# V in 32 KB runs: two kv heads of four batches in one tile, 64 stationary columns, 0/1 masks on P

## The chip, the cores and the metric

The kernel runs on one core of a Trainium2 chip. The metric is the device time of one execution in microseconds; each figure is the median of several executions. Five engines work side by side and wait for one another through semaphores: TensorE (PE in the profile, its weight loads PEld), VectorE (DVE), ScalarE (ACT), GpSimd (POOL) and SyncE (SP). SP issues nearly all of this kernel's transfers in program order; 16 DMA engines carry them out.

## The reference: one decode step of attention beside an MLP

Four sequences (B = 4) have one new token each, with D = 576. The result is `x + A(xn) + B(xn)`, `xn` being the layer norm of `x`.

A is attention over the last W = 2048 of 8192 cached positions, with 32 query heads, 16 kv heads (each serves rep = 2 query heads) and 128 numbers per head:

```
q = xn @ wq                       # 4 x 32 heads x 128
scores = q . k * 128**-0.5        # over 2048 positions
p = softmax(scores)
o = p @ v                         # 4 x 32 x 128
A = o.reshape(4, 4096) @ wo
```

B is `x1 + gelu(layernorm(x1) @ w3) @ w4` with F = 4608. Its first part, which shifts h = gelu(layernorm(x) @ w1) along the sequence before `@ w2`, shifts everything out, as there is one position only, so w1 and w2 are not read.

What must be read is 33.6 MB of K, 33.6 MB of V, 4.7 MB each of wq and wo, and 5.3 MB each of w3 and w4, all in bf16: 87.2 MB in all.

## The kernel before, in words

**Tiles and buffers.** The pool `big` has four buffers of 32 KB per partition, 4 MB each. In turn they hold wq, the K tiles, w3, the V tiles and the end of w4. The pool `kt` has two buffers of 16 KB per partition, `pz` one and `wo` two. A load into a buffer waits, on SP, until the last reader of what the buffer held is done, and every later load stands behind it in SP's queue.

**K and the scores.** Eight K tiles come in, 4 MB each; a partition's row is one run of 32 KB. DVE transposes each in blocks of 32 x 32 (L297), PE multiplies with the queries (L304), and scores of all heads and positions stand in four PSUM banks, `S[0..3]`, one row per (kv head, batch, query head) and 512 columns each.

**Softmax (L309 to L356).** DVE takes the maximum (L316 to L318). ACT makes the exponentials in eight instructions of 256 columns, into the f32 tile `E`, with row sums on the way (L321). DVE takes the reciprocal of the sum (L325, L326) and multiplies it with a mask that says to which batch a row belongs (`rdm`, L328). Then, for each of four pieces of 16 columns, `E` is multiplied with the four columns of `rdm`, three times on DVE (L342) and once on ACT (L340), which gives one copy for each batch, normalized, with zeros in the other batches' rows (`prs`, bf16). PE transposes these (L346), and DVE (L354) and ACT (L351) copy the result from PSUM to `PZ`. `PZ` holds, for each kv head, 64 chunks of 8 columns (4 batches x 2 query heads).

**V.** A V tile holds two kv heads. Each head is one DMA of 2 MB (L122): a partition is a (position block, batch), 32 blocks of 64 positions by 4 batches, so its row is a run of 64 x 128 bf16 = 16 KB. `v_compute(h)` (L384) makes 16 matmuls per head, each with 32 stationary columns of `PZ` (4 chunks x 8 columns) and 512 moving columns of V (4 chunks x 128). They go to four column tiles of 32 in turn; a column tile is a group of 32 PSUM partitions. The blocks on the diagonal, where the chunk of P meets the same chunk of V, are the ones wanted. `head_out(h)` adds up the four diagonal blocks with the 0/1 columns of `diag` (L413 once, L415 three times).

**Behind V.** `transpose_sum` (L425, L427) transposes the sum, adding up over partitions on the way. After every fourth head `select` rearranges four heads' outputs with the matrix `pick` (L436, eight matmuls) and four pairs of small DVE operations (L443, L444), and `project` multiplies them with a group of rows of wo (L395, 16 matmuls). In the loop over v (L545 on) PE's order is written out by hand: `run_projects` (the project of the group before), `v_compute(v)`, then `transpose_sum` and perhaps `select` of head v - 1. SP's order: four V tiles and two wo groups before the softmax, then one V tile after each second head, the third and fourth wo group behind v = 5 and v = 9, and last w4's remaining rows in five DMAs (`w_end`, L482).

**The end.** The last select, the last project, and w4's last rows (L504, four column tiles) go to three accumulators; `sums` and `perm` (L566 to L572) bring them together, and `fin` (L579) goes out.

Of the kernel before, what the change touches and what calls it, by code (L numbers as in the profile page):

```python
# [8 lines left out]
ACT = mybir.ActivationFunctionType  # L9
ALU = mybir.AluOpType  # L10
AX = mybir.AxisListType
BF16 = mybir.dt.bfloat16
F32 = mybir.dt.float32
# [7 lines left out]
def kernel(  # L21
# [30 lines left out]
    NCH = W // G  # L52
    NG = P // G
    GK = G // B
    NY = 4
    CP = 16
    NP = NCH // CP
    assert NCH * GK == 512
# [12 lines left out]
    v_win = A_v_cache[:, :, Sk - W:Sk, :]  # L71
# [46 lines left out]
    def v_load(pair):  # L118
        t = big.tile([P, 2, NCH, Dh], BF16, tag="big", name=f"v{pair}")
        for i in range(2):  # L120
            h = 2 * pair + i
            nc.sync.dma_start(out=t[:, i, :, :].rearrange("p c d -> p (c d)"),  # L122
                              in_=v_win[:, h].rearrange("b (p c) d -> p b (c d)", p=G))
            V_tiles[h] = t[:, i, :, :]
# [5 lines left out]
    wo_src = A_wo.rearrange("(g p x) n -> p g (x n)", p=P, x=XR)  # L130
# [42 lines left out]
    xn_f = const.tile([B, D], F32)  # L173
# [27 lines left out]
    mask = const.tile([P, B], F32)  # L201
    nc.vector.tensor_reduce(out=mask[:], in_=ident[:].rearrange("p (h b r) -> p b h r", b=B, r=rep), op=ALU.add, axis=AX.XY)
# [105 lines left out]

    def softmax():  # L309

        E = ktp.tile([P, NCH, NG, GK], F32, tag="kt", name="E")
        mx = const.tile([P, NG], F32)
        nb = const.tile([P, 1], F32)
        sm = const.tile([P, 2 * NG], F32)
        for g in range(NG):
            nc.vector.reduce_max(out=mx[:, g:g + 1], in_=S[g][:], axis=AX.X)  # L316
        nc.vector.reduce_max(out=nb[:], in_=mx[:], axis=AX.X)
        nc.vector.tensor_scalar_mul(out=nb[:], in0=nb[:], scalar1=-scale)  # L318
        for g in range(NG):
            for x in range(2):  # L320
                nc.scalar.activation(out=E[:, :, g, x:GK:2].rearrange("p (c l) q -> p c q l", l=2),  # L321
                                     in_=S[g][:, 256 * x:256 * (x + 1)].rearrange("p (c q l) -> p c q l", q=4, l=2),
                                     func=ACT.Exp, bias=nb[:], scale=scale, accum_out=sm[:, 2 * g + x:2 * g + x + 1])
        rd = const.tile([P, 1], F32)
        nc.vector.tensor_reduce(out=rd[:], in_=sm[:], op=ALU.add, axis=AX.X)  # L325
        nc.vector.reciprocal(out=rd[:], in_=rd[:])  # L326
        rdm = const.tile([P, B], F32)
        nc.vector.tensor_scalar_mul(out=rdm[:], in0=mask[:], scalar1=rd[:])  # L328

        PZ = pzp.tile([P, Hkv, NCH, B * rep], BF16, tag="pz", name="PZ")  # L330
        HC = CP // 2
        prs = ktp.tile([P, NP, CP, NG, GK, B], BF16, tag="kt", name="prs")
        for piece in range(NP):
            c0 = piece * CP
            pr = prs[:, piece]
            for b in range(B):
                src = E[:, c0:c0 + CP, :, :].rearrange("p c g k -> p (c g k)")
                dst = pr[:, :, :, :, b].rearrange("p c g k -> p (c g k)")
                if b == 3:
                    nc.scalar.mul(out=dst, in_=src, mul=rdm[:, b:b + 1])  # L340
                else:
                    nc.vector.tensor_scalar_mul(out=dst, in0=src, scalar1=rdm[:, b:b + 1])  # L342
            for half in range(2):
                tp = ps_s.tile([P, HC, P], BF16, tag="S", name=f"pt{piece}{half}")
                for cc in range(HC):
                    nc.tensor.transpose(out=tp[:, cc, :],  # L346
                                        in_=pr[:, half * HC + cc, :, :, :].rearrange("p g k b -> p (g k b)"),
                                        identity=ident[:])
                c1 = c0 + half * HC
                if half:  # L350
                    nc.scalar.copy(out=ap_of(PZ, c1 * B * rep, [[NCH * B * rep, Hkv], [B * rep, HC], [1, B * rep]]),  # L351
                                   in_=ap_of(tp, 0, [[B * rep, Hkv], [P, HC], [1, B * rep]]))
                else:
                    nc.vector.tensor_copy(out=ap32(PZ, c1 * B, [[NCH * B, Hkv], [B, HC], [1, B]]),  # L354
                                          in_=ap32(tp, 0, [[B, Hkv], [NH * B // 2, HC], [1, B]]))
        return PZ  # L356


    NI = 4
    NB = B * rep  # L360
    sel = const.tile([P, NB], F32)
    nc.vector.tensor_reduce(out=sel[:], in_=ident[:].rearrange("p (q m) -> p m q", m=NB), op=ALU.add, axis=AX.X)
    diag = const.tile([P, NI], F32)
    nc.vector.tensor_reduce(out=diag[:], in_=ident[:].rearrange("p (j i m) -> p i j m", i=NI, m=NB), op=ALU.add,
                            axis=AX.XY)

    pick = const.tile([P, XR, 2, P // XR], BF16)
    for j in range(2):
        nc.vector.tensor_copy(out=pick[:, :, j, :], in_=ident[:].rearrange("p (m x) -> p x m", x=XR))

    half = const.tile([P, 2], F32)
    nc.vector.tensor_reduce(out=half[:], in_=ident[:].rearrange("p (q j m) -> p j q m", j=2, m=16), op=ALU.add, axis=AX.XY)
    O_tiles = {}

    def v_compute(h):
        bank = ps_o.tile([P, NI * Dh], F32, tag="O", name=f"O{h}")
        vn = V_tiles.pop(h)
        g0, m = divmod(h, NM)
        hp = 4 * (m % 4) + 2 * (m // 4) + g0
        ns = NCH // (NI * NG)  # L380
        for s in range(ns):
            for j in range(NG):
                c0 = (s * NG + j) * NI
                nc.tensor.matmul(out=bank[G * j:G * j + G, :],  # L384
                                 lhsT=PZ[:, hp, c0:c0 + NI, :].rearrange("p c m -> p (c m)"),
                                 rhs=vn[:, c0:c0 + NI, :].rearrange("p c d -> p (c d)"),
                                 start=(s == 0), stop=(s == ns - 1), skip_group_check=True)
        O_tiles[h] = bank
# [11 lines left out]
    NO = 4  # L400

    def load_wo(g2):
        wo_tiles[g2] = wop.tile([P, XR, D], BF16, tag="wo", name=f"wo{g2}")
        nc.sync.dma_start(out=wo_tiles[g2][:].rearrange("p x n -> p (x n)"), in_=wo_src[:, g2, :])
# [3 lines left out]
    def head_out(h):  # L408


        bank = O_tiles.pop(h)
        osum = ktp.tile([P, Dh], F32, tag="kt", name=f"osum{h}")
        nc.vector.tensor_scalar_mul(out=osum[:], in0=bank[:, 0:Dh], scalar1=diag[:, 0:1])  # L413
        for i in range(1, NI):
            nc.vector.scalar_tensor_tensor(out=osum[:], in0=bank[:, i * Dh:(i + 1) * Dh], scalar=diag[:, i:i + 1],  # L415
                                           in1=osum[:], op0=ALU.mult, op1=ALU.add)

        g4, o = divmod(h, NO)

        def transpose_sum():  # L420
            if o == 0:
                OT = ps_tp.tile([P, NO * NB * (1 + XR)], F32, tag="tp", name=f"OT{g4}")
                groups[g4] = OT, small.tile([P, NO, rep, B], BF16, tag="on", name=f"on{g4}")
            OT, on = groups[g4]
            nc.tensor.matmul(out=OT[:, NB * o:NB * o + NB], lhsT=osum[:], rhs=sel[:], start=True, stop=True,  # L425
                             skip_group_check=True)
            nc.vector.tensor_copy(out=on[:, o].rearrange("p r b -> p b r"),  # L427
                                  in_=OT[:, NB * o:NB * o + NB].rearrange("p (b r) -> p b r", r=rep))

        def select():  # L430
            if o < NO - 1:
                return
            OT, on = groups.pop(g4)
            T = OT[:, NO * NB:].rearrange("p (x n) -> p x n", x=XR)
            for x in range(XR):
                nc.tensor.matmul(out=T[0:32, x, :], lhsT=pick[:, x, :, :].rearrange("p j m -> p (j m)"),  # L436
                                 rhs=on[:].rearrange("p o r b -> p (o r b)"),
                                 start=(x == 0), stop=(x == XR - 1), skip_group_check=True)
            onx = small.tile([P, XR, B], BF16, tag="onx", name=f"onx{g4}")
            tmp = small.tile([32, NO, XR, B], F32, tag="tmp", name=f"tmp{g4}")  # L440
            for q in range(NO):
                n = NB * q
                nc.vector.tensor_scalar_mul(out=tmp[:, q], in0=T[0:32, :, n + B:n + 2 * B], scalar1=half[0:32, 1:2])  # L443
# [93 lines left out]
    PZ = softmax()  # L537

    with tc.manual_schedule(engines={mybir.EngineType.PE}):
# [5 lines left out]
        for v in range(Hkv):  # L545
            run_projects()
            v_compute(v)
# [4 lines left out]
            head_out(v)  # L552

            if v in (5, 9):
                load_wo((v + 3) // 4)
            if v % 2 and v // 2 + NV0 < Hkv // 2:
                v_load(v // 2 + NV0)
# [7 lines left out]
        sums = ktp.tile([P, DH], F32, tag="kt", name="sums")  # L565
# [45 lines left out]
```

## Time and profile before

| | |
|---|---|
| median of three runs | 213.44 us (213.19 to 213.72) |
| span of the profiled execution, first to last instruction | 212.0 us; the median lies 1.4 us above it |
| HBM read | 87.17 MB, 411 GB/s over the span |
| busy PE, DVE, ACT | 98.4, 128.2, 17.4 us (46, 60, 8%) |
| last K tile's transposes | end at 121.4 us |
| softmax, from the last scores to the first V matmul | 123.4 to 140.3 us |
| V matmuls (L384) | 140.3 to 199.1 us, 256 of them |
| last landing of w_end | 208.35 us |

The profile is one execution on the chip. Its second part cuts the span into 40 slices of 5.3 us; a digit is the busy share in tenths, and DMA is the mean share of the 16 engines. A group's row gives line, engine, operation, output <- inputs, shapes and count, then busy time and mean duration of one, then the engine's idle time ahead of it and what ended that. In the timeline, a row gives start, duration and what ran; a bracket at the end gives the idle time ahead and what ended it. The chain that ended last goes through V's landings (15% of the span) and w_end's (10%).

PEclk is the granted TensorE clock. Ahead of its first record, at 137.7 us, the row shows full speed, though the bursts of 16 score matmuls there take 1.90 us, the same as bursts of 16 V matmuls take later where the row says 0.5.

### The profile page before, as it was taken

How to read it: one execution, taken by the hardware profiler on the slowest of the kernel's cores; microseconds unless marked ns; L12 is line 12 of the kernel's file. 1: busy time of each engine (PE TensorE's matmuls, PEld its weight loads, DVE VectorE, ACT ScalarE, POOL GpSimd, SP SyncE). 2: the span in 40 equal slices, each digit the busy share in tenths (PEclk: the TensorE clock that was granted, in tenths of full speed). 3: DMA queues.
4: the chain of work that ended last, by engine and by line, in shares of the span. 5: the costliest groups of instructions: out<-in, count | busy, mean ns of one | idle time of the engine just before them, and what ended most of it. 6: DMA issues, size and time to landing. Idle time of an engine off the chain costs nothing. (4 is left out here: it accounts for less than half of the span.)

```text
span 212.0 us, 2539 instructions
## 1 busy us (share of the span) xinstructions
PE 98.4 (46%) x1071; PEld 50.5 (24%) x1071; DVE 128.2 (60%) x225; ACT 17.4 (8%) x35; POOL 1.8 (1%) x8
## 2 busy tenths in 40 slices
PE   1442059429903333423333421968573644555573
PEld 0111027408301011101111101734231321212241
DVE  7812592095349898979699916968475322145240
ACT  0004100000000000000000058730000000000000
POOL 2100000000000000000000000000000000000000
PEclk9999999999999999999999999999787555555555
DMA  7999999999999999999999999999999999999980
GB/s 261 427 457 433 411 442 454 392 420 460 420 420 457 411 445 433 408 451 399 433 427 420 436 415 432 436 423 423 426 430 417 434 415 438 423 427 419 423 356 18
DMA packets 5943, 87.32 MB, mean 412 GB/s; under 512 B 681, under 2 KB 685, under 8 KB 1453
## 3 DMA queue, kind: packets, MB, share of 16 engines
q1 hardware_dynamic: 5924, 87.17, 96.8%
q8 instruction: 8, 0.13, 0.3%
q14 instruction: 3, 0.02, 0.0%
q10 hardware_dynamic: 8, 0.00, 0.0%
HBM read 87.17 MB, written 0.00 MB: 411 GB/s over the span
## 5 line engine op out<-in xcount | busy, mean ns | idle before, releaser
L297 DVE STREAM_TRANSPOSE kt<-k 128x2048 int32<-128x2048 int32 x32 | 71.0, 2278 | 17.5 <-DMA k<-in_A_k_cache_dram 17.5
L304 PE MATMUL S<-kt,qz 128*32 128x512 bf16 x256 | 30.4, 622 | 56.9 <-DVE kt L297 56.9
L384 PE MATMUL O<-v,PZ 128*32 128x512 bf16 x256 | 23.6, 506 | 15.1 <-DMA v<-in_A_v_cache_dram 15.1
L304 PEld LDWEIGHTS <-qz 128*32 128x32 bf16 x256 | 9.5, 127 | 74.0 <-issue 67.5
L413 DVE TENSOR_SCALAR osum<-O,diag 128x128 f32<-128x128 f32 x16 | 5.6, 348 | 28.8 <-PE O L384 28.8
L415 DVE SCALAR_TENSOR_TENSOR osum<-O,diag,osum 128x128 f32<-128x128 f32 x48 | 16.5, 345 | 0.9
L384 PEld LDWEIGHTS <-PZ 128*32 128x32 bf16 x256 | 7.5, 116 | 22.5 <-DMA v<-in_A_v_cache_dram 12.6
L346 PE MATMUL pt<-ident,prs 128*128 128x128 bf16 x64 | 6.5, 287 | 10.1 <-DVE prs L342 10.1
L321 ACT ACTIVATE E<-S,nb 128x256 f32<-128x256 f32 x8 | 4.5, 704 | 69.9 <-DVE nb L318 69.9
L425 PEld LDWEIGHTS OT<-sel,osum 128*128 128x128 f32 x32 | 6.6, 258 | 13.5 <-issue 7.1
L425 PE MATMUL OT<-sel,osum 128*128 128x8 f32 x32 | 8.1, 326 | 3.4 <-DVE osum L415 3.4
L395 PE MATMUL ACC<-wo,onx 128*4 128x288 bf16 x64 | 4.5, 434 | 8.7 <-DVE onx L444 8.7
L346 PEld LDWEIGHTS <-prs 128*128 128x128 bf16 x64 | 5.8, 131 | 11.5 <-ACT prs L340 9.4
L342 DVE TENSOR_SCALAR prs<-E,rdm 128x512 bf16<-128x512 f32 x12 | 7.8, 801 | 0.0
L465 PEld LDWEIGHTS <-w3a 128*128 128x128 bf16 x108 | 6.9, 161 | 1.7 <-issue 1.7
L465 PE MATMUL ACC<-ln2T,w3a 128*128 128x4 bf16 x108 | 7.0, 202 | 0.0
L316 DVE TENSOR_REDUCE mx<-S 128x1 f32<-128x512 f32 x4 | 2.7, 681 | 5.4 <-PE S L304 5.4
L236 PE MATMUL qp<-wq,xnT 128*8 128x512 bf16 x32 | 3.8, 621 | 4.5 <-DMA wq<-in_A_wq_dram 4.5
L567 ACT COPY sums<-ACC 64x288 f32<-64x288 f32 x1 | 0.4, 393 | 64.5 <-PE ACC L395 64.5
L251 DVE CAST q_rows<-qp 128x256 bf16<-128x256 f32 x4 | 1.5, 420 | 5.9 <-PE qp L236 3.9
L340 ACT ACTIVATE prs<-E,rdm 128x512 bf16<-128x512 f32 x4 | 4.9, 1404 | 0.8 <-DVE rdm L328 0.8
L465 PEld LDWEIGHTS <-w3b 128*128 128x128 bf16 x72 | 4.5, 160 | 0.8 <-issue 0.8
(91 smaller groups left out, 68.1 us busy)
## 6 DMA issues: line engine op xcount, KB each, us to landing
v<-in_A_v_cache_dram SPq DMA_DIRECT2D x16, 2048.0 KB, 26.4
k<-in_A_k_cache_dram SPq DMA_DIRECT2D x7, 4096.0 KB, 30.6
wo<-in_A_wo_dram SPq DMA_DIRECT2D x4, 1152.0 KB, 29.8
wq<-in_A_wq_dram SPq DMA_DIRECT2D x2, 2048.0 KB, 12.9
k<-in_A_k_cache_dram SPq DMA_DIRECT2D x2, 2048.0 KB, 25.0
w3a<-in_B_w_dram SPq DMA_DIRECT2D x1, 2304.0 KB, 27.0
w3b<-in_B_w_dram SPq DMA_DIRECT2D x1, 2304.0 KB
w3b<-in_B_w_dram SPq DMA_DIRECT2D x1, 1728.0 KB, 34.6
```

Source lines behind the costliest of these rows:

```text
L297: nc.vector.transpose(out=ap32(kt[e], c0 * 2 * G, [[2 * G, C2 // 2], [1, 2], [2, G]]), in_=ap32(kn, c0 * 4 * G + e * G, [[4 * G, C2 // 2], ...
L304: nc.tensor.matmul(out=S[kq][c:c + 32, :].rearrange("p (c q l) -> p c q l", q=4, l=2), lhsT=qz[:, bp, m, y, :], rhs=kt[e][:, :, 4 * m:4 * ...
L321: nc.scalar.activation(out=E[:, :, g, x:GK:2].rearrange("p (c l) q -> p c q l", l=2), in_=S[g][:, 256 * x:256 * (x + 1)].rearrange("p (c q ...
L340: nc.scalar.mul(out=dst, in_=src, mul=rdm[:, b:b + 1])
L342: nc.vector.tensor_scalar_mul(out=dst, in0=src, scalar1=rdm[:, b:b + 1])
L346: nc.tensor.transpose(out=tp[:, cc, :], in_=pr[:, half * HC + cc, :, :, :].rearrange("p g k b -> p (g k b)"), identity=ident[:])
L384: nc.tensor.matmul(out=bank[G * j:G * j + G, :], lhsT=PZ[:, hp, c0:c0 + NI, :].rearrange("p c m -> p (c m)"), rhs=vn[:, c0:c0 + NI, :].rea ...
L395: nc.tensor.matmul(out=ACCS[half][o0:o0 + B, 0:DH], lhsT=lhsT, rhs=rhs_cols(q * DH, (q + 1) * DH), start=False, stop=False, skip_group_che ...
L413: nc.vector.tensor_scalar_mul(out=osum[:], in0=bank[:, 0:Dh], scalar1=diag[:, 0:1])
L415: nc.vector.scalar_tensor_tensor(out=osum[:], in0=bank[:, i * Dh:(i + 1) * Dh], scalar=diag[:, i:i + 1], in1=osum[:], op0=ALU.mult, op1=AL ...
L425: nc.tensor.matmul(out=OT[:, NB * o:NB * o + NB], lhsT=osum[:], rhs=sel[:], start=True, stop=True, skip_group_check=True)
L465: nc.tensor.matmul(out=gp[:, fc, :], lhsT=lhsT, rhs=rhs, start=False, stop=False, skip_group_check=True)
```

## The change

A V tile still holds two kv heads of all four batches, but a partition is now (position block, batch, which head): 16 blocks of 128 positions, so that a row is a run of 128 x 128 bf16 = 32 KB, and the tile is one DMA of 4 MB (the last tile: three, with runs of 16, 8 and 8 KB). The two heads are i and i + 8. A chunk of P has 16 columns, 2 heads x 4 batches x 2 query heads, with zeros where batch or head of the row is another. So `PZ` doubles, to two tiles of 16 KB per partition, PZ0 in the pool `kt` and PZ1 in `pz`.

- **Masks.** Constants from the identity: `of_batch`, `of_side`, the mask for each batch and head (0/1), `of_pair`, `of_col`, another `diag`.
- **Softmax.** Four exponentials of 512 columns, bf16, into `EP`. For each of eight pieces, eight multiplies on DVE by a 0/1 mask, bf16 to bf16, 256 numbers per partition, into one of three scratch areas of `EP`; 16 transposes on PE; two copies from PSUM (DVE and ACT; both on ACT for the pieces 2 and 5).
- **Normalizing.** The reciprocal of the sums is taken after the first piece, spread over columns, and brought by a small matmul (`RD`) to the layout of V's output. Multiplied with `diag` it is `dsel`, which takes `diag`'s place behind V.
- **V.** 32 matmuls per pair, 64 stationary columns (4 chunks x 16), two column tiles of 64 in turn.
- **Behind V.** `pair_out` per pair instead of `head_out` per head, with the same four DVE operations, for half as many sums; `transpose_sum` gives 16 columns at once; `select` and `project` after every second pair, with the rows of wo in another order. The sums of all pairs and `sums` lie in one tile, `OS`.
- **Order.** One V tile is loaded after each of the first four pairs, wo groups 2 and 3 behind pairs 3 and 5.

```diff
-    v_win = A_v_cache[:, :, Sk - W:Sk, :]
+    v_win = A_v_cache[:, :, Sk - W:Sk, :].rearrange("b (h i) (p c) d -> i p b h (c d)", h=2, p=KP)
...
-    def v_load(pair):
-        t = big.tile([P, 2, NCH, Dh], BF16, tag="big", name=f"v{pair}")
-        for i in range(2):
-            h = 2 * pair + i
-            nc.sync.dma_start(out=t[:, i, :, :].rearrange("p c d -> p (c d)"),
-                              in_=v_win[:, h].rearrange("b (p c) d -> p b (c d)", p=G))
+    def v_load(pair, cuts=(CK,)):
+        t = big.tile([P, CK, Dh], BF16, tag="big", name=f"v{pair}")
+        c0 = 0
+        for n in cuts:
+            a, z = c0 * Dh, (c0 + n) * Dh
+            nc.sync.dma_start(out=t[:].rearrange("p c d -> p (c d)")[:, a:z], in_=v_win[pair][:, :, :, a:z])
+            c0 += n
...
-            for x in range(2):
-                nc.scalar.activation(out=E[:, :, g, x:GK:2].rearrange("p (c l) q -> p c q l", l=2),
...
+            nc.scalar.activation(out=ap_of(EP, 4 * g * CK, [[2, CK // 2], [CK, 4], [1, 2]]),
+                                 in_=S[g][:].rearrange("p (c q l) -> p c q l", q=4, l=2),
+                                 func=ACT.Exp, bias=nb[:], scale=scale, accum_out=sm[:, g:g + 1])
...
-                if b == 3:
-                    nc.scalar.mul(out=dst, in_=src, mul=rdm[:, b:b + 1])
-                else:
-                    nc.vector.tensor_scalar_mul(out=dst, in0=src, scalar1=rdm[:, b:b + 1])
+        for piece in range(CK // CP):
+            off = KP * CK * (1 + piece % 3)
+            for v in range(NV):
+                nc.vector.tensor_scalar_mul(out=ap_of(EP, off + v * CP, [[NV * CP, KP], [1, CP]]),
+                                            in0=ap_of(EP, piece * CP, [[CK, KP], [1, CP]]),
+                                            scalar1=mask[:, v // 2, v % 2:v % 2 + 1])
...
+                if half or piece in (2, 5):
+                    nc.scalar.copy(out=ap_of(t, c1 * NW, [[CH * NW, Hkv // 2], [NW, HC], [1, NW]]),
...
+            if piece == 0:
+                rd = const.tile([P, 1], F32)
+                nc.vector.tensor_reduce(out=rd[:], in_=sm[:], op=ALU.add, axis=AX.X)
+                nc.vector.reciprocal(out=rd[:], in_=rd[:])
+                spread = xn_t[:, 0:P]
+                nc.vector.tensor_scalar_mul(out=spread.rearrange("p (k n) -> p k n", n=NW),
+                                            in0=ap_of(of_col, 0, [[0, P // NW], [1, NW]]), scalar1=rd[:])
+                RD = ps_tp.tile([P, Hkv // 2], F32, tag="tp", name="RD")
+                nc.tensor.matmul(out=RD[:], lhsT=spread, rhs=of_pair[:], start=True, stop=True,
+                                 skip_group_check=True)
+                nc.vector.tensor_tensor(out=dsel[:], in0=ap_of(diag, 0, [[0, Hkv // 2], [1, NI]]),
+                                        in1=ap_of(RD, 0, [[1, Hkv // 2], [0, NI]]), op=ALU.mult)
...
-                nc.tensor.matmul(out=bank[G * j:G * j + G, :],
-                                 lhsT=PZ[:, hp, c0:c0 + NI, :].rearrange("p c m -> p (c m)"),
+                nc.tensor.matmul(out=bank[64 * j:64 * j + 64, :],
+                                 lhsT=PZ[c0 // CH][:, of, c0 % CH:c0 % CH + NI, :].rearrange("p c n -> p (c n)"),
...
-            head_out(v)
-
-            if v in (5, 9):
-                load_wo((v + 3) // 4)
-            if v % 2 and v // 2 + NV0 < Hkv // 2:
-                v_load(v // 2 + NV0)
+            pair_out(i)
+
+            if i in (3, 5):
+                load_wo((i + 1) // 2)
+            if i + NV0 < Hkv // 2:
+                v_load(i + NV0, (CH, CH // 2, CH // 2) if i + NV0 == Hkv // 2 - 1 else (CK,))
```

## The prediction

> **What bounds the kernel now.** I read the slices of the span first, then the DMA queue in stretches with one kind of run each, then SP's issues, then the timeline of the V stage and of the end.
>
> ```profile
> PEclk9999999999999999999999999999787555555555
> DMA  7999999999999999999999999999999999999980
> ```
>
> The 16 DMA engines are full from the second slice to the second last; no compute engine is (DVE 60%, PE 46%). So the time is bytes over rate, as long as SP issues early enough and nothing drags on behind the last landing. Two stretches with one kind of run each, 55 to 95 us (K, 32 KB runs) and 98.5 to 126 us (V, 16 KB runs), from the view of the DMA queues:
>
> ```profile
> DMA packets 591, 17.25 MB, mean 431 GB/s; under 512 B 64, under 2 KB 64, under 8 KB 64
> ...
> q1 hardware_dynamic: 590, 17.24, 100.2%
> ```
> ```profile
> DMA packets 800, 11.71 MB, mean 426 GB/s; under 512 B 85, under 2 KB 85, under 8 KB 85
> ...
> q1 hardware_dynamic: 799, 11.70, 100.0%
> ```
>
> Both are full, at different speeds. K: 16 engines x 40 us x 1.002 = 641.3 us for 590 - 64 = 526 long packets, 1.219 us each. V: 440.0 us for 714, 0.616 us each, 1.232 us for two. The same bytes cost 13 ns less as one run; V at 132 to 149, 155 to 171 and 177 to 193 us gives 0.617 to 0.618 each, so 15 to 17. I take 15.
>
> How far ahead SP is, and how little room the end has, stands in the timeline:
>
> ```profile
> 142.32 4.79 SPq L122 DMA_DIRECT2D v<-in_A_v_cache_dram  x4
> ...
> 160.13 1.05 PE L384 MATMUL O<-v,PZ 128*32 128x512 bf16 x16 [2.06 <-DMA v<-in_A_v_cache_dram]
> ```
> ```profile
> 152.27 1.92 PE L384 MATMUL O<-v,PZ 128*32 128x512 bf16 x16
> ...
> 154.65 1.09 PE L384 MATMUL O<-v,PZ 128*32 128x512 bf16 x16
> ...
> 182.49 1.90 PE L384 MATMUL O<-v,PZ 128*32 128x512 bf16 x16 [5.25 <-DMA v<-in_A_v_cache_dram]
> ...
> 188.03 1.13 PE L395 MATMUL ACC<-wo,onx 128*4 128x288 bf16 x16 [2.48 <-DVE onx L444]
> ...
> 188.94 1.92 PE L384 MATMUL O<-v,PZ 128*32 128x512 bf16 x16
> ...
> 197.17 1.90 PE L384 MATMUL O<-v,PZ 128*32 128x512 bf16 x16 [2.46 <-DMA v<-in_A_v_cache_dram]
> ...
> 206.59 0.79 PE L504 MATMUL ACC<-w_end,gTq 128*32 128x144 bf16 x20
> ...
> 207.68 0.55 PE L504 MATMUL ACC<-w_end,gTq 128*32 128x144 bf16 x12 [0.30 <-DMA w_end<-in_B_w_dram]
> ...
> 208.39 0.43 PE L504 MATMUL ACC<-w_end,gTq 128*32 128x144 bf16 x8 [0.16 <-DMA w_end<-in_B_w_dram]
> ```
>
> Head 15 lands at 197.17 us; its burst ends at 199.07. From there PE and DVE work nearly without a pause to 207.38; 20 matmuls more, at the pace of the 20 before (0.79 us), make 208.2. They really end at 208.82, held by two last landings. So the stream sets the end with only 0.6 us to spare.
>
> **The change, part by part.**
>
> *Runs.* 2048 V packets of 16 KB (128 per engine) become, per engine, 56 of 32 KB, 8 of 16 KB and 16 of 8 KB (the last pair's cuts). 56 x 15 ns = 0.84 us less; the 8 KB pieces pay half of 15 ns more on 8 pairs, 0.06. **Sum -0.8 us**; bounds 0 and 64 x 17 ns = 1.1 us. [...]
>
> *V matmuls.* Still 256 of 512 columns, but on two column tiles instead of four. A burst of 16 takes 1.90 us at clock 0.5: 0.107 us each, a quarter of 0.43, so four run abreast; at full clock 1.05, 0.053 each. Two abreast, a pair's 32 matmuls take 6.8 us at half clock and 3.4 at full, where two heads took 3.6 to 3.8 and 2.0. A pair lands every 9.8 us (4.19 MB at 427 GB/s), so in mid-stage this is hidden; it counts in the first pair, whose buffer the next load waits for, and at the end. No abreast running at all (13.7 us) is the far bound; I take two.
>
> *Softmax.* The rows:
>
> ```profile
> L346 PE MATMUL pt<-ident,prs 128*128 128x128 bf16 x64 | 6.5, 287 | 10.1 <-DVE prs L342 10.1
> ...
> L342 DVE TENSOR_SCALAR prs<-E,rdm 128x512 bf16<-128x512 f32 x12 | 7.8, 801 | 0.0
> ```
> ```profile
> L168 DVE TENSOR_SCALAR xn_f<-x_bf,mv,rstd 4x576 f32<-4x576 bf16 x1 | 0.6, 567 | 0.1
> ...
> L168 DVE TENSOR_SCALAR ln_bf<-xn_bf,mv,rstd 4x576 bf16<-4x576 bf16 x1 | 0.4, 418 | 0.3 <-POOL rstd L166 0.3
> ```
>
> Eight exponentials of 256 (4.6 us) become four of 512: the spacing of 0.55 us grows by 256 elements x about 0.8 ns to 0.76, 3.2 us in all; and the sum, reciprocal and mask (0.6 us) leave the path. So the multiplies start near 127.8 instead of 129.8 us. Twelve DVE and four ACT multiplies of 512 become 64 on DVE of 256 bf16. L342 is spaced 0.606 us (seven in 4.24) with 0.97 ns per element (from L277 and L471: 729 and 309 ns for 576 and 144), so about 0.11 fixed. L168 shows 149 ns less for bf16 out than for f32 out; if that is a halving, bf16 to bf16 costs 0.26 ns per element: 0.07 + 0.11 = 0.17 us, or 0.14 by the least fixed share. [...] I take 0.16, since L168 is the only dense bf16 row: 10.2 us. Copies from PSUM: 6 of 0.51 on DVE (3.1), 10 of 1.0 on ACT, beside them. 128 transposes: 0.107 us each at half clock, 13.7 in all, half that once the clock is up; PE starts with piece 0 at 129 and stays just inside DVE's pace. New wait: PE's RD matmul waits for sum, reciprocal and spread on DVE, with piece 1's transposes queued behind it and DVE behind those: 1.0 us. Last piece: 1.5. So V starts at 127.8 + 10.2 + 3.1 + 1.0 + 1.5 = 143.6, where it was 140.3. Pair 0 then takes 3.5 us (clock up after the transposes), and SP issues pair 4 at 147.1 instead of 142.3. What that meets: the queue in front of head 8 ran until about 155 on the slowest engine (160.1 less 4.9 us for 2.1 MB), some 3 us less on the fastest (the share falls from 1.00 at 200 to 205 us to 0.47 at 205 to 208, so engines finish apart); with 1 to 2 us from issue to first bytes the last safe issue is near 150. **Cost 0**, cover about 3 us.
>
> *The rest.* The added reductions on the identity (some six of 216 to 356 ns, 1.5 us) run before 12 us, where DVE idles 3.9 us for the q matmuls. DVE loses half of 64 sums from PSUM (11 us) off the path. wo 2 moves behind pair 6 in SP's queue, wo 3 and w_end are issued a few us later, over 20 us ahead of use: 0.
>
> *The end.* Stream alone: 208.8 - 0.8 = 208.0. Compute: the last V piece lands at 196.4. Back over pair 7 (9.8) and wo 2 (2.8), pair 6 lands at 183.8. Then pair 6's burst, then 4.6 us of sums, select and project (184.32 to 188.94 before), then pair 7's burst, then 9.1 to the last matmul. All at half clock: 183.8 + 6.9 + 4.6 + 6.9 + 9.1 = 211.3. All at full clock: pair 7 waits for its last quarter, 196.4 + 0.9 + 9.1 = 206.4. Between: 3.4 us of unbroken work from 151.36 brought the burst from 1.92 back to 1.09, and a 6.8 us burst is unbroken, so each speeds up on its way and takes about 5 to 6 us; some stretch of full clock also carries over from the project before it. That is 183.8 + 5.3 + 4.6 + 5.0 = 198.7, + 9.1 = 207.8: level with the stream. [...]
>
> **Sum.** Span 212.0 - 0.8 = 211.2, a tenth for an end that is level. The median lies 1.4 us over the profiled span, so 212.7 us.
>
> **Rivals.**
> - *TensorE sets the end.* Bursts stay mostly at half clock (for it: clock 0.50 throughout 170 to 208 us; against: 32 matmuls in a row, not 16). End 208.5 to 211.3, time 213.1 to 215.9.
> - *The queue runs dry at 150 us (slower).* Place: SP's wait for pair 0's matmuls. It decides from 0.20 us per multiply. [...] At 0.21, or with 2 to 5 us of extra stalls among DVE, PE and ACT over the three scratch areas and four PSUM banks: 213 to 215. [...]
> - *The runs bring nothing*, because the two heads of a packet row lie far apart, or the 1% is K's layout: 213.4 with the end as before. Against: K's runs lie far apart too.
>
> **Chances.** Forecast (212.3 to 212.9) 0.43; TensorE at the end 0.27; queue dry 0.20; no gain 0.10. About 0.3% (0.64 us) is what a measurement tells from no change: below 212.8 with 0.40, between 212.8 and 214.1 with 0.28 (half of the second, most of the fourth, a little of the first and third), above with 0.32. Range 212.3 to 216.2.
>
> **What would show it.** Right: V packets of 1.22 us, multiplies spaced 0.14 to 0.18, pair 4 issued before 150, DMA share 1.00 from 145 to 160, and the last matmuls waiting for w_end. Wrong: a hole in the DMA row after 150, pair 4 issued later than that, or the last w_end matmuls without a DMA wait and the project behind pair 7 later than 204.

## The result and the profile after

The changed kernel takes **300.7 us** where the kernel before takes 213.6 on the same chip. Four of its six executions, the profiled one among them, were over 1.5% slower than the fastest; the two fast ones (295.65 and 297.63 us) give 1.389 times the time before, with a 95% interval of 1.385 to 1.393. The forecast was 212.7, the top of the range 216.2. The profiled execution after took 301.18 us, its span is 299.4.

The slices of the changed kernel's span and its main DMA queue, from the page:

```profile
PEclk9999999955555555559978557568557568576757
DMA  8999999999999999999899999899999999999991
GB/s 307 464 420 426 439 402 442 420 438 440 433 425 433 412 306 225 206 215 215 185 252 204 223 215 219 183 250 201 219 215 228 225 215 193 223 224 230 265 388 44
...
q1 hardware_dynamic: 5060, 87.17, 97.3%
```

Read the DMA row and the GB/s row together. The 16 engines are busy to the end, as before, so there is no hole and no engine that lets the stream wait. But from slice 14 on (105 us, where V follows K) they move some 215 GB/s instead of some 430. A busy DMA row says that packets are in flight, not that they are fast. The same 87.17 MB kept the engines busy for 0.968 x 212.0 = 205.2 us before and for 0.973 x 299.4 = 291.3 us after. These 86.1 us are nearly all of the 87.4 us by which the span grew.

The main queue in a stretch with V alone, 162 to 184 us of the changed kernel (packets, MB, share of the 16 engines' time):

```profile
q1 hardware_dynamic: 160, 4.72, 99.9%
```

4.72 MB are 144 runs of 32 KB, and 16 x 22 us x 0.999 over 144 is **2.44 us** each, where K's runs of the same length take 1.22 and two of the old 16 KB runs took 1.23. That is 1.21 us on each of 64 pairs of old runs per engine, 77 of the 86 us. The rest is not separated; wo's and w_end's packets run among them.

The timeline of the changed kernel (start, duration, engine, instruction, count, and in brackets the wait ahead of it):

```profile
124.56 0.69 ACT L345 ACTIVATE EP<-S,nb 128x512 bf16<-128x512 f32 x1 [69.97 <-DVE nb L343]
...
127.38 1.66 DVE L353 TENSOR_SCALAR EP<-EP,mask 128x256 bf16<-128x256 bf16 x8 [2.90 <-ACT EP L345]
...
145.85 3.64 PE L400 MATMUL O<-v,PZ 128*64 128x512 bf16 x32
149.53 8.64 SPq L122 DMA_DIRECT2D v<-in_A_v_cache_dram  x2
152.28 5.33 PE L400 MATMUL O<-v,PZ 128*64 128x512 bf16 x32 [2.78 <-DMA v<-in_A_v_cache_dram]
...
177.79 6.43 PE L400 MATMUL O<-v,PZ 128*64 128x512 bf16 x32 [19.85 <-DMA v<-in_A_v_cache_dram]
...
295.77 0.43 PE L520 MATMUL ACC<-w_end,gTq 128*32 128x144 bf16 x8 [0.15 <-DMA w_end<-in_B_w_dram]
```

Up to 149.53 us the compute runs within 2.5 us of the forecast. After that TensorE waits for V, up to 20 us at a time. So the question for the experiments was one of DMA alone: why does a 32 KB packet of V take twice as long as one of K?

### The profile page after: what moved, and what is told of

Same layout as the page of the kernel before. It is cut to its first block, busy times and chain, and to the rows that moved or that the text cites. A ratio compares the mean times of both kernels' runs of the same rounds, so it can differ in the third digit from the quotient of the medians.

```text
span 299.4 us, 2645 instructions
## 1 busy us (share of the span) xinstructions
PE 119.6 (40%) x1121; PEld 64.6 (22%) x1121; DVE 124.5 (42%) x244; ACT 16.7 (6%) x29; POOL 1.8 (1%) x8
## 3 DMA queue, kind: packets, MB, share of 16 engines
q1 hardware_dynamic: 5060, 87.17, 97.3%
HBM read 87.17 MB, written 0.00 MB: 291 GB/s over the span
## 4 chain that ended last, share of the span: by engine, by line
another core or an unknown queue 30%; PE 14%; DVE 9%; DMA 7%; ACT 1%; issue 1%; SPq 1%; ACTq 0%
PE O L400 9%; DMA w_end<-in_B_w_dram 7%; DVE kt L312 4%; PE pt L359 3%; DVE EP L353 2%; ACT EP L345 1%; PE ACC L411 1%; DVE PZ L367 1%; PE S L319 1%; DVE tmp L459 1%; DVE onx L460 1%; SPq L498 1%; DVE OS L431 0%; ACT PZ L364 0%
## 5 line engine op out<-in xcount | busy, mean ns | idle before, releaser
L400 PE MATMUL O<-v,PZ 128*64 128x512 bf16 x256 | 44.0, 516 | 82.7 <-DMA v<-in_A_v_cache_dram 82.7
L400 PEld LDWEIGHTS <-PZ 128*64 128x64 bf16 x256 | 20.7, 146 | 104.4 <-issue 57.1
L359 PE MATMUL pt<-ident,EP 128*128 128x128 bf16 x128 | 11.5, 258 | 10.3 <-DVE rd L371 5.7
L353 DVE TENSOR_SCALAR EP<-EP,mask 128x256 bf16<-128x256 bf16 x64 | 13.4, 280 | 2.9 <-ACT EP L345 2.9
L359 PEld LDWEIGHTS <-EP 128*128 128x128 bf16 x128 | 10.3, 154 | 12.1 <-DVE EP L353 12.1
L364 ACT COPY PZ<-pt 128x1024 bf16<-128x1024 bf16 x10 | 9.8, 1015 | 9.4 <-PE pt L359 9.2
L431 DVE SCALAR_TENSOR_TENSOR OS<-O,dsel,OS 128x128 f32<-128x128 f32 x24 | 8.2, 343 | 0.4
L481 PE MATMUL ACC<-ln2T,w3b 128*128 128x4 bf16 x72 | 4.6, 202 | 0.0
L367 DVE COPY PZ<-pt 128x512 int32<-128x512 int32 x6 | 4.1, 692 | 1.1 <-PE pt L359 1.0
L459 DVE TENSOR_SCALAR tmp<-OT,half 32x32 f32<-32x32 f32 x16 | 3.8, 237 | 1.1 <-PE OT L452 1.0
```

The costliest lines, as they stand in the source:

```text
L353: nc.vector.tensor_scalar_mul(out=ap_of(EP, off + v * CP, [[NV * CP, KP], [1, CP]]), in0=ap_of(EP, piece * CP, [[CK, KP], [1, CP]]), scala ...
L359: nc.tensor.transpose(out=tp[:, cc, :], in_=ap_of(EP, off + half * HC + cc, [[CP, P]]), identity=ident[:])
L364: nc.scalar.copy(out=ap_of(t, c1 * NW, [[CH * NW, Hkv // 2], [NW, HC], [1, NW]]), in_=ap_of(tp, 0, [[NW, Hkv // 2], [P, HC], [1, NW]]))
L367: nc.vector.tensor_copy(out=ap32(t, c1 * NB, [[CH * NB, Hkv // 2], [NB, HC], [1, NB]]), in_=ap32(tp, 0, [[NB, Hkv // 2], [P // 2, HC], [1, ...
L400: nc.tensor.matmul(out=bank[64 * j:64 * j + 64, :], lhsT=PZ[c0 // CH][:, of, c0 % CH:c0 % CH + NI, :].rearrange("p c n -> p (c n)"), rhs=v ...
L431: nc.vector.scalar_tensor_tensor(out=osum, in0=bank[:, k * Dh:(k + 1) * Dh], scalar=dsel[:, of, k:k + 1], in1=osum, op0=ALU.mult, op1=ALU.add)
```

## The experiments

Five theories, by the letters that the expectations use. **A**: rows far apart in memory (16 MB between heads i and i+8) are slow to read. **B**: blocks 32 KB apart, read at once, are slow. **C**: the change's own compute slows the transfers beside it. **D**: the write side; what counts is which partitions of on-chip memory are written at the same moment, and 16 blocks of 8 neighbouring partitions make a slow set. **E**: an order with 16 blocks outermost is slow in itself, wherever it is written.

**Loads alone, ten orders (m1_orders).** Nothing of the reference is computed; four tiles of 4 MB per order. The three that matter, as dimensions from the outermost to the run:

```
x2m   [[32 KB, 16], [2 MB, 8],  [32 KB run]]    # 16 blocks, rows 2 MB apart; x4m, x8m, x16m likewise
mq    [[2 MB, 32],  [32 KB, 4], [32 KB run]]    # the order of K
p16k  [[16 KB, 32], [32 MB, 4], [16 KB run]]    # V's order in the kernel before
```

Of the others shown below, p32k is p16k with blocks 32 KB apart; p16k_x16m has 16 KB runs in 16 blocks with rows 16 MB apart; halves has 16 blocks x 4 rows, 32 MB apart, written to partitions 0 to 63 and then to 64 to 127.

> Loads alone: ten orders of reading V, four tiles of 4 MB each, one after the other on SP, four buffers, no compute but one copied column per tile (the output is zeros). Full rate is 9.8 us a tile, 39 us an order; the rate of the changed kernel (216 GB/s) is 19.5 and 78. [...] Theory B (blocks 32 KB apart, read in step, use half of the memory): every order with blocks 32 KB apart is slow, that with 16 KB runs 32 KB apart too; K's order and that of before are fast, and blocks 64 KB apart are no better. Theory C (compute takes the ports): all ten take 39 us.

The lines view: the last column is the time that DVE waited for the four tiles of an order.

```profile
L59 DVE COPY seen<-x16m 128x1 bf16<-128x1 bf16 x4 | 0.6, 156 | 81.8 <-DMA x16m<-in_A_v_cache_dram 81.8
L64 DVE COPY seen<-x2m 128x1 bf16<-128x1 bf16 x4 | 0.6, 156 | 79.2 <-DMA x2m<-in_A_v_cache_dram 79.2
...
L84 DVE COPY seen<-p16k 128x1 bf16<-128x1 bf16 x4 | 0.6, 156 | 33.6 <-DMA p16k<-in_A_v_cache_dram 33.6
L89 DVE COPY seen<-p32k 128x1 bf16<-128x1 bf16 x4 | 0.6, 156 | 38.5 <-DMA p32k<-in_A_v_cache_dram 38.5
L94 DVE COPY seen<-p16k_x16m 128x1 bf16<-128x1 bf16 x4 | 0.6, 156 | 73.5 <-DMA p16k_x16m<-in_A_v_cache_dram 73.5
L79 DVE COPY seen<-mq 128x1 bf16<-128x1 bf16 x4 | 0.6, 156 | 38.1 <-DMA mq<-in_A_v_cache_dram 38.1
L99 DVE COPY seen<-halves 128x1 bf16<-128x1 bf16 x4 | 0.6, 156 | 89.3 <-DMA halves<-in_A_v_cache_dram 89.3
```

A falls: 2 MB and 16 MB between rows differ by 3% (4 MB, 8 MB and blocks 64 KB apart: 79.0 to 79.2 us), and K's order, rows 2 MB apart too, is twice as fast. B falls: "p32k" reads blocks 32 KB apart at full rate. C falls: no engine computes here. What the slow orders share is 16 blocks outermost, with 8 rows each or, in "halves", with 4 rows written to partitions 0 to 63 and then 64 to 127. The orders at full rate have 32 blocks or rows outermost and 4 inside. The run length is not what makes an order slow (16 KB runs with 16 blocks: 73.5 us). D and E are left.

**The changed kernel with V read in K's order (e1_k_order, e1_again).**

```diff
-in_=v_win[pair][:, :, :, a:z]        # 16 blocks x (4 batches x 2 heads)
+in_=src[:, :, a:z]                   # K's: 32 rows of (b, h) x 4 blocks
```

> The changed kernel whole, but V's tiles are read in the order of K's tiles (32 rows of batch and head, four blocks of 32 KB each), so masks and P meet other rows of V than the reference's; bytes, run length (32 KB) and every instruction beside the source addresses are the same. Theories A and B: V packets of 1.22 us and the time that the prediction gave without the slow packets, 212 to 216 us (SP issued pair 4 at 149.5 us, so that the queue may have a hole of 0 to 2 us). Theory C: stays near 300 us.

213.59 us against 213.59 before, ratio 0.9987 (0.9969 to 1.0005). Its queue from 155 to 171 us:

```profile
q1 hardware_dynamic: 226, 6.88, 100.0%
```

6.88 MB are 210 runs of 32 KB, 1.22 us each. Everything else that the change does is in this kernel, so **the whole loss comes from the order of this one transfer**. It too leaves the theories D and E.

**The kernel before with the changed kernel's order (e2_before_far).**

```diff
-in_=v_win[:, h].rearrange("b (p c) d -> p b (c d)", p=G)
+in_=v_far[pair][:, :, :, i * NCH * Dh:(i + 1) * NCH * Dh]    # 16 blocks x 8 rows, half a run each
```

> The kernel before, whole, but each of a tile's two transfers reads 16 KB runs in the changed kernel's order (16 blocks 32 KB apart, eight rows 16 MB apart), so heads and positions are mixed up. Theories A and B: packets of 16 KB take about 1.19 us, twice as long, and the time is about 295 to 300 us, with nothing of the change's compute in it. Theory C: stays at 213.4 us.

298.62 us, one execution. From 162 to 184 us its 16 KB packets take 1.19 us (4.85 MB, 296 runs, 0.998 of the engines' time). The GB/s row of its page has the same step at slice 14 and 15, with 16 KB runs and the old softmax:

```profile
GB/s 306 469 429 384 437 437 460 424 429 427 424 424 429 416 340 210 219 219 230 210 237 228 223 219 223 219 232 214 232 224 221 224 209 230 226 219 224 247 378 31
```

**Loads alone, the same source written to other partitions (m2_ports).** Nothing of the reference is computed. The shape 16 blocks x 4 rows goes to 64 partitions, and only the first partition changes:

```
nc.sync.dma_start(out=t[0:64, :],   in_=src_of([[32 KB, 16], [32 MB, 4], [32 KB run]]))   # L57, waited for in L58
nc.sync.dma_start(out=t[32:96, :],  in_=...the same...)                                    # L61, L62
nc.sync.dma_start(out=t[64:128, :], in_=...the same...)                                    # L65, L66
# L69 and L73: 32 blocks x 2 rows to 0..63 and to 32..95
# L77 to L94, all 128 partitions: 128 rows (L79), 64 blocks x 2 rows (L84), and two queues,
#   each half of the partitions (L89) or half of each run (L94)
```

> Loads alone again (the output is zeros), nine orders, 16.8 MB each, runs of 32 KB: 39 us at full rate, 78 at half. The first look at loads refuted theories A, B and C: every order of 16 blocks was slow, whatever the distance of the rows, every order of 32 blocks was fast. [...] Theory E (16 in the outermost place of the source is slow in itself): the first three all 78, the two with 32 in the outermost place 39. [...]

The lines view, with the wait in the last column (for eight transfers of 2 MB in the first five lines, for 16.8 MB in the others as well), and the queue in a stretch of L57 (10 to 70 us) and of L61 (88 to 106 us):

```profile
L66 DVE COPY seen<-s16x_at 32x1 bf16<-32x1 bf16 x8 | 1.2, 147 | 80.5 <-DMA s16x_at<-in_A_v_cache_dram 80.5
L62 DVE COPY seen<-s16x_at 32x1 bf16<-32x1 bf16 x8 | 1.2, 146 | 37.8 <-DMA s16x_at<-in_A_v_cache_dram 37.8
L74 DVE COPY seen<-s32x_at 32x1 bf16<-32x1 bf16 x8 | 1.2, 146 | 37.7 <-DMA s32x_at<-in_A_v_cache_dram 37.7
L70 DVE COPY seen<-s32x_at 32x1 bf16<-32x1 bf16 x8 | 1.2, 144 | 80.9 <-DMA s32x_at<-in_A_v_cache_dram 80.9
L58 DVE COPY seen<-s16x_at 32x1 bf16<-32x1 bf16 x8 | 1.2, 144 | 82.9 <-DMA s16x_at<-in_A_v_cache_dram 82.9
L89 DVE COPY seen<-two_q_parts 128x1 bf16<-128x1 bf16 x4 | 0.6, 157 | 66.9 <-DMA two_q_parts<-in_A_v_cache_dram 66.9
L94 DVE COPY seen<-two_q_runs 128x1 bf16<-128x1 bf16 x4 | 0.6, 156 | 61.9 <-DMA two_q_runs<-in_A_v_cache_dram 61.9
L84 DVE COPY seen<-s64x 128x1 bf16<-128x1 bf16 x4 | 0.6, 156 | 73.4 <-DMA s64x<-in_A_v_cache_dram 73.4
L79 DVE COPY seen<-s 128x1 bf16<-128x1 bf16 x4 | 0.6, 156 | 38.2 <-DMA s<-in_A_v_cache_dram 38.2
```
```profile
q1 hardware_dynamic: 464, 12.06, 98.3%
```
```profile
q1 hardware_dynamic: 303, 7.83, 101.2%
```

12.06 MB are 368 runs: 2.56 us each. 7.83 MB are 239: 1.22 us. Same source, same shape, same queue; only the partitions written differ. **E falls, and what D says of partitions stands for transfers to 64 of them.** 64 to 127 are slow again: from 135 to 180 us, within L65's transfers, 9.31 MB are 284 runs in 1.012 of 16 x 45 us, 2.57 us each. Why 0 to 63 and 64 to 127 are slow and 32 to 95 are not, no run shows.

64 blocks x 2 rows (L84) waited 73.4 us. Their first tile landed 9.6 us behind the last of L79, which is the full rate; from 375.18 us on ACT's queue wrote to partitions 64 to 127 beside the other three, and they took 21 to 22 us each. So one tile alone shows 64 x 2. The two orders with two queues waited 66.9 and 61.9 us, between the full rate's 39 and the half's 78.

How the partitions can make a transfer to all 128 of them slow is not shown: which engine writes which partition is not in the trace, and 16 x 8 in one transfer to other partitions was not run. The next experiments test D by its consequences.

**The changed kernel with V on other partitions (e5_swapped_pool, e6_swapped_sp).** Same runs, same masks and sums, P written to match.

```diff
-nc.sync.dma_start(out=tf[:, a:z], in_=v_win[pair][:, :, :, a:z])
+nc.sync.dma_start(out=tf[32:96, a:z], in_=v_win[pair][:, :, 0, a:z])
+nc.gpsimd.dma_start(out=tf[0:32, a:z], in_=v_win[pair][0:8, :, 1, a:z])      # e6: nc.sync
+nc.gpsimd.dma_start(out=tf[96:128, a:z], in_=v_win[pair][8:16, :, 1, a:z])   # e6: nc.sync
```

> The changed kernel whole, computing the same output from the same 32 KB runs; only which partition a run lies on is changed. The first head of a tile goes to partitions 32 to 95 (block times 4 plus batch), by SP's queue in one transfer of 16 blocks x 4 rows, the shape and place that ran at 1.216 us per packet in the loads measured alone. The second head goes to partitions 0 to 31 and 96 to 127 in two transfers of 8 blocks x 4 rows from POOL's queue, and the softmax multiplies write P in the same arrangement. [...] If both go to the same eight engines, these have 12 packets per tile instead of 8: 14.6 us per tile instead of 9.8, some 250 us. Rival (the source's order, 16 blocks outermost in a whole kernel, is slow wherever it is written): packets of 2.5 us and 300 us.

> The same as the kernel with the second head in two transfers of 8 blocks x 4 rows, but these two are issued by SP as well. Theory D with transfers of 8 blocks going to the same eight engines each time: eight engines have 12 packets per tile and eight have 4, each packet 1.22 us, so 14.6 us per tile, 39 us more over eight tiles: about 252 us, with DMA busy share near 0.67 in the V stage. If SP's transfers of 8 blocks are spread over all 16 engines: 213 to 214.5. Rival (source's order): 300.

e5: 221.67 us, ratio 1.0377 (1.0344 to 1.0410). Its two queues from 98 to 126 us (q1 is SP's, with the last of K and the first of V; q0 is POOL's, V alone):

```profile
q1 hardware_dynamic: 385, 6.73, 56.4%
q0 software_dynamic: 371, 5.24, 43.9%
```

POOL's 5.24 MB are 160 runs in 0.439 of 16 x 28 us: 1.23 us each. SP's 6.73 MB are by bytes 205 runs of 32 KB, 1.23 too. So the rate is back, against the rival's 300 us, with the source still in the order that was slow. The time is still 8 us over the kernel before. One cause is seen in the DMA row and the timeline of e5:

```profile
DMA  7999999999999999999999999996498999999930
```
```profile
129.50 0.69 ACT L348 ACTIVATE EP<-S,nb 128x512 bf16<-128x512 f32 x1 [74.99 <-DVE nb L346]
...
155.47 7.92 SPq L123 DMA_DIRECT2D v<-in_A_v_cache_dram  x3
```

POOL's transfers run beside the last K tiles, which land 5 us later; so the exponentials start at 129.50 instead of 124.56, pair 4 is issued at 155.47 instead of 149.53, and the queues stand empty before it (the 6 and 4 in the row).

e6: 267.9 us. From 165 to 195 us its one queue shows

```profile
q1 hardware_dynamic: 375, 8.51, 70.6%
```

0.71 of the engines' time busy, 284 GB/s, 14.8 us for a tile of 4.19 MB: as eight engines with 12 packets per tile would have it (0.67 and 14.6). Which engines carry a transfer is not in the trace. That SP's transfers of eight blocks all go to the same eight engines is the author's estimate from these two numbers; that POOL's two do not, from e5, where the two queues together fill 0.564 + 0.439 = 1.00 of the engines' time. The whole of e6 is 16 us over the expected 252; from 205 us on, with the last pair in nine transfers, it moves only 235 GB/s, and I have not followed that.

**POOL's transfers behind K (e7_pool_after_k, e8_pool_behind_k, e9_pool_in_order).**

```diff
+nc.gpsimd.tensor_copy(out=k_seen[:], in_=kf[:, BIG - 1:BIG])            # pair 0; e7: no k_seen, straight from the K tile
+nc.gpsimd.tensor_copy(out=tf[0:32, a:a + 1], in_=k_seen[0:32])          # e7, e8: pairs 0 to 3; e9: 0 to 2
+nc.gpsimd.tensor_copy(out=tf[96:128, a:a + 1], in_=k_seen[96:128])
```

> The kernel with V on swapped partitions and the second head on POOL's queue (221.67 us) with one more wait: POOL copies an element of the last K tile into each of the first four V tiles before it loads into them, so its transfers start behind the last K tile. Theory: the 8 us that kernel lost are POOL's V transfers running beside the last K tiles (exponentials at 129.50 instead of 124.56 us, pair 4 issued at 155.5 instead of 149.5 us, then 5 us without data); with them gone exponentials are back at 124.6, pair 4 is issued by 150, no hole follows, and the time is 212.8 to 214.0, as with V in K's order. Rival (two queues in themselves cost stream rate in the V stage): still 218 to 222 with no hole at 151 to 157 us but a rate below 420 GB/s over the V stage.

> As the last kernel, but the element of the last K tile goes once into a small tile of its own and from there into the first four V tiles, so that no V tile waits for a buffer that another V tile's copy still holds (the fourth V tile had waited for pair 0's matmuls until 149.9 us, and the queues stood empty from 142 to 151 us). Theory: exponentials at 124.5 us, pair 4 issued by 150 us, no hole, V packets 1.22 to 1.25 us as in the first kernel with POOL's queue, and 212.8 to 214.5 in all. [...] Rival (two queues in themselves cost stream rate): 218 to 222 with packets above 1.3 us throughout V.

> As the last kernel, without the copy into the fourth V tile, so that POOL issues the second heads pair after pair, 0 to 31 and 96 to 127 in turn (in the last kernel pair 4's first transfer stood ahead of pair 3's, which waited for pair 0's matmuls with it, and two transfers to partitions 0 to 31 were issued in a row; packets were 1.74 and 1.98 us from 156 to 176 us, where in strict turn they had been 1.23). Theory: exponentials at 125 us, pair 4 issued by 150 us, no hole of over 2 us, packets of 1.22 to 1.28 us in all of V, and 213 to 215 in all. Rival (two queues in themselves cost stream rate, or POOL's transfers finish late at the end): 216 to 222, with packets above 1.3 us, or with the last pair's burst more than 3 us later than in the kernel with V in K's order (194.65 us).

e7: 245.22 us, ratio 1.1513 (1.1470 to 1.1555); e8: 235.29, 1.1014 (1.0983 to 1.1046). In both the exponentials were back at 124.4 to 125.1 us, but by the waits POOL issued pair 4's first transfer ahead of pair 3's, and pair 3 waited for pair 0's matmuls with it. My reading of e7 (a buffer held too long) was wrong; e8 took that away (in e7 the queues had stood empty from 142 to 151 us) and kept the order. That order makes a test of D: two transfers to the same partitions in a row. POOL's issues in e8 and the queues from 156 to 176 us:

```profile
150.59 1.06 POOL L132 DMA_DIRECT2D v<-in_A_v_cache_dram  x2 [28.82 <-PE O L413]
151.64 1.08 POOL L133 DMA_DIRECT2D v<-in_A_v_cache_dram  x2
```
```profile
q1 hardware_dynamic: 153, 3.97, 66.0%
q0 software_dynamic: 156, 1.93, 36.5%
```

Two transfers to partitions 0 to 31 (L132) in a row, then two to 96 to 127 (L133). 121 runs of q1 take 1.74 us each and 59 of q0 1.98. In e9, in strict turn, the queues from 126 to 150 us:

```profile
q0 software_dynamic: 394, 5.28, 51.9%
q1 hardware_dynamic: 310, 5.24, 51.2%
```

By bytes these are 161 and 160 runs of 32 KB (a load of wo is among SP's), at 1.24 and 1.23 us. From 156 to 176 us e9 moves 424 GB/s, where e8 moved 296. The same transfers to the same partitions, issued in another order, cost half as much again (1.74 and 1.98 us a run against 1.23 and 1.24): what counts is which partitions are written **at the same moment**, as D says. e9 takes 219.31 us, ratio 1.0255 (1.0236 to 1.0275), with a DMA row that is full to the last but two slices. The 213 to 215 of its expectation missed, and the rival that POOL's transfers finish late came true: of the 8 us of e5, the transfers beside K explain some 2.4. The stream is repaired; what is late there is the end:

```profile
DMA  7999999999999999999999999999999999999900
```
```profile
191.05 5.33 PE L413 MATMUL O<-v,PZ 128*64 128x512 bf16 x32 [3.25 <-DMA v<-in_A_v_cache_dram]
...
200.39 2.78 PE L413 MATMUL O<-v,PZ 128*64 128x512 bf16 x24
...
204.60 1.05 PE L413 MATMUL O<-v,PZ 128*64 128x512 bf16 x8 [1.43 <-DMA v<-in_A_v_cache_dram]
```
```profile
170.74 0.53 POOL L132 DMA_DIRECT2D v<-in_A_v_cache_dram  x1 [2.69 <-DMA v<-in_A_v_cache_dram]
174.76 0.53 POOL L133 DMA_DIRECT2D v<-in_A_v_cache_dram  x1 [3.49 <-DMA v<-in_A_v_cache_dram]
181.37 0.53 POOL L132 DMA_DIRECT2D v<-in_A_v_cache_dram  x1 [6.08 <-DMA v<-in_A_v_cache_dram]
183.30 0.53 POOL L133 DMA_DIRECT2D v<-in_A_v_cache_dram  x1 [1.40 <-DMA v<-in_A_v_cache_dram]
```

The last pair's burst starts at 200.39 us (194.65 in e1_k_order) and its last piece at 204.60. SP issues its share of that pair from 166.72 us on, POOL from 166.99 on; but each of POOL's last four transfers waits for an earlier landing of V, and the last is issued at 183.30, among w_end's on SP's queue. The last burst ends at 205.65, where the kernel before ended its own at 199.07; these 6.6 us are about the 5.7 us of the time and the 0.6 us that the end had to spare. Why POOL waits for landings there, no run shows. A version with the reference's output, the long runs and a time below the kernel before was not reached.

**The gain alone and the end (e4_runs_alone, e3_late_pe).**

```diff
# e4: the kernel before
-in_=v_win[:, h].rearrange("b (p c) d -> p b (c d)", p=G)      # two transfers of 16 KB runs
+in_=src[:, :, a * n:(a + 1) * n]                              # K's order, 32 KB runs
# e3: V in K's order, half of the matmuls of pairs 6 and 7 left out
-ns = CK // (NI * NJ)
+ns = CK // (NI * NJ) // (2 if i > 5 else 1)
```

> The kernel before, with 32 KB runs alone: V tiles read in K's order, one transfer of 4 MB each (the last in two, 16 KB runs), four column tiles, softmax and all else as before (P meets other rows of V than the reference's). By the prediction's first term: 7 x 8 pairs of packets per engine x 15 ns = 0.84 us less, 212.7 us, since here TensorE stays in time. If longer runs bring nothing: 213.5.

> The changed kernel with V in K's order (as in the run above, 213.59 us) and with half of the V matmuls of the last two pairs left out, so TensorE's bursts there are half as long (the left-out half of V's positions is missing from the sums). If TensorE's late end is what eats the gain of the longer runs: the last matmuls wait for w_end again and the time falls to 212.5 to 212.8 (0.8 us below before, less than half of 1%). If the transfers themselves did not get faster, or the queue had a hole behind the softmax: stays at 213.4 to 213.6.

> V in K's order in the changed kernel once more (the masks then meet other V rows), in more rounds, beside the kernel that computes the reference's output from V on swapped partitions. The first time: 213.59 against 213.59, ratio 0.9969 to 1.0005. If the run length brings what the kernel before showed alone (ratio 0.9965) and late TensorE work takes most of it back, 0.9975 to 0.9995 here, 213.0 to 213.5; if nothing is taken back, 0.9965.

e4: 212.90 us, ratio **0.9965** (0.9953 to 0.9978), 0.7 us less. (That is the median without one execution of 335.94 us, in which the 256 score matmuls took 87 us in place of 30; the profile is of that one and is not used further.) It has nine V transfers in place of sixteen, so run length and number of transfers change together. e1_again: 213.00 us, 0.9982 (0.9967 to 0.9997), within its range. e3: 213.02 us, 0.9978 (0.9969 to 0.9988), between the two values of its expectation and no faster than e1_again. The end of e1_again and of e3 in the timeline:

```profile
193.28 5.93 PE L404 MATMUL O<-v,PZ 128*64 128x512 bf16 x32
...
206.32 1.42 PE L524 MATMUL ACC<-w_end,gTq 128*32 128x144 bf16 x40
```
```profile
191.83 3.43 PE L404 MATMUL O<-v,PZ 128*64 128x512 bf16 x16 [0.21 <-DMA v<-in_A_v_cache_dram]
...
207.27 1.13 PE L524 MATMUL ACC<-w_end,gTq 128*32 128x144 bf16 x20 [0.24 <-DMA w_end<-in_B_w_dram]
```

In e1_again the last matmuls wait for no DMA and end at 207.74: TensorE is the end. The same holds in the profile of e1_k_order, where they end at 209.29. With fewer V matmuls (e3) w_end is. That fits a compute end level with the stream, but the intervals of e1_again, e3 and e4 touch, so how much of the 0.7 us the two-abreast matmuls take back is not shown.

## Why the prediction was wrong, point by point

- **What bounds the kernel**: right. Bytes over rate, before and after; after, at half the rate in V (some 215 GB/s for some 430).
- **Runs, -0.8 us: the step that failed.** The size of the gain was right (e4: -0.7). What failed is that K's 1.219 us was taken for V's new rows, as if run length were all that a packet's time depends on; the runs showed 2.44 us for the same 32 KB, by which partitions are written together. The reshaped load was a third shape, 16 blocks x 8 rows, of which the trace of before has no row: K has 32 x 4, V had 32 x 4. The term came out as +86 us of busy DMA time, 77 of them counted in V's packets. My text held the unknown between 0 and 1.1 us of gain; nothing in it allowed a loss, though a shape without a row needs a bound on both sides.
- **The rival "the runs bring nothing"**: it named the place, a packet row of two far heads, but the wrong mechanism. Distance in memory is not the cause (m1_orders: 79.2 us at 2 MB, 81.8 at 16 MB). And the argument against it, that K's rows lie far apart too, was true and beside the point: it compared sources, and what differs is which partitions are written together.
- **V matmuls, two abreast**: right. 3.64 us at a granted clock of 1.00 (3.4 to 3.5 said), 4.9 to 6.4 as the clock rises within a burst (5 to 6 said, 6.8 the bound): in the burst at 177.79 us it is 0.50 up to 183 us and 0.80 in the 1.2 us behind that. 3.64 us are 0.11 us a matmul; in the kernel before, two of 512 columns that are not abreast (L541, L544) start 0.22 us apart, at 139.76 and 139.98 us, also at 1.00.
- **Softmax**: nearly right. The multiplies start at 127.38 (127.8 said) and are spaced 0.197 us from start to start (0.16 said; eight take 1.66, the last of them 0.28). Read in the same way, L342's rows are spaced 0.573 us: the 0.606 of the prediction has the length of the last one in it. The six copies on DVE take 0.69 us each (0.51 said). V starts at 145.85 (143.6 said), pair 4 is issued at 149.53 (147.1 said). The cover held: with V in K's order pair 4 goes out at 149.75 and no hole follows.
- **The rival "queue dry"**: its point of decision, 0.20 us per multiply, was just not reached at 0.197. Pair 4 went out at 149.53 to 149.97 us, just ahead of the 150 that it gave as the last safe time, and the queue did not run dry. What a late issue does is seen in e5: issued at 155.47, the queues stand empty before it.
- **The end**: the size was right, the order in part. Level with the stream, 207.8 said for the last matmul; with V in K's order it came at 207.74 (e1_again) and at 209.29 (e1_k_order), both times without a wait for w_end. So TensorE set the end there, as the rival of that name has it. The 208.5 at that rival's lower end no run shows; the runs showed these two.
- **What would show it**: the first mark, V packets of 1.22 us, failed at 2.44, and the second, multiplies spaced 0.14 to 0.18, at 0.197. The three others (DMA share 1.00 from 145 to 160, pair 4 before 150, the last matmuls waiting for w_end) all held in a kernel 41% over the forecast. Marks on shares and order do not see a packet that is slow.

## What to carry to other kernels

When a load is reshaped, compare both ends of it with a load that the trace has: not only the run length and the source, but which partitions the engines write at one moment. With 16 parts outermost and 8 neighbouring partitions in each, the rate was half (215 GB/s); with 32 x 4 (431 GB/s), 128 rows (38.2 us for four tiles), 16 x 4 from partition 32 on (37.8 us), and in one tile 64 x 2 (9.6 us), it was full. Look at GB/s beside the DMA row: 9s there stood beside 430 GB/s and beside 215, and say only that something is in flight.

## What the runs showed of the hardware

- A run of 32 KB into on-chip memory takes 1.22 us or 2.44 to 2.56 us, a run of 16 KB 0.616 or 1.19. Of the causes tried, only the partitions that are written together fit every run: 16 blocks x 8 rows at 128 partitions 215 GB/s, 32 x 4 of the same bytes 425 to 431.
- 64 partitions are as fast as 128 if they are 32 to 95 (eight transfers of 2 MB in 37.8 us of waiting, as four of 4 MB in K's order in 38.1), and half as fast if they are 0 to 63 or 64 to 127 (82.9 and 80.5).
- Rows 2, 4, 8 or 16 MB apart in memory read equally fast at half rate (79.1 to 81.8 us). At full rate only 2 MB (38.1 us) and 32 MB (33.6 to 38.5 us) were run.
- Runs of 32 KB to partitions 0 to 31 and 96 to 127, in two transfers of eight blocks from POOL's queue beside SP's to 32 to 95, take 1.23 to 1.24 us when the two are issued in turn (e5, e9), and 1.98 us, with 1.74 on SP's queue, when two to the same partitions follow each other (e8).
